# Which DMA ring carries the first weights of a fused layer norm, SSM and SwiGLU kernel, and in which order their first products run

## The chip, the cores and the metric

The kernel runs on one core of a Trainium2 chip. The metric is the device time of one execution in microseconds (us). Times inside an execution come from its profile and are counted from the start of its span; the engines are called as the profile calls them: PE (TensorE, matmuls), DVE (VectorE), ACT (ScalarE), POOL (GpSimd) and SP (SyncE). SPq and ACTq are the instruction streams of SP and ACT in their part as issuers of DMAs; each of the two has a DMA ring of its own.

## The reference

The input `x` has 2048 rows of 512 bf16 values. All matrices are bf16.

```python
xn = _layernorm(x, axis=-1)                       # eps 1e-5, no scale, no shift
# A: a diagonal complex state space layer, 512 states, a scan over the 2048 rows
Bu = einsum("bld,pd->blp", xn, B_bar)
h  = Lam_bar * h + Bu[:, t]                       # for t in 0..2047
yA = 2 * einsum("blp,dp->bld", hseq, Cmat).real + xn * Dskip
# B: SwiGLU, F = 1792
yB = (silu(xn @ w1) * (xn @ w3)) @ w2
return x + yA + yB
```

## The kernel before

The rows are handled in four blocks of 512 (`NBLK`), each of four chunks of 128 rows (c0 to c3 of the first block here). For the products the normalised rows have to stand transposed, 512 features on the partitions in four groups of 128 (`dt` 0 to 3); this is `xnT`. The hidden width 1792 is cut into 14 tiles of 128 (`f`). `glu_up` makes, for each f, a gate product with `w1` (into a PSUM tile `g_ps`) and an up product with `w3` (into `u_ps`); ACT takes both out of PSUM, DVE multiplies. `ssm_in`, the scan tasks and `y_out` do the rest. DVE's tasks of the main part come from a queue with costs in us (`push`, `drain`); nothing of that is touched.

The first block has a head of its own, written out by hand as one program order for each engine (the lines after `stats(0)` at the end of the kernel):

- **Transfers.** SP issues x's chunk c0, then c1 (128 KB each, L77), then four pieces of 256 KB, the first four f tiles of w1 and w3 by halves of the contraction: w1 low (dt 0 and 1), w1 high (dt 2 and 3), w3 low, w3 high (L95); then larger pieces of w1 and w3 (512 and 768 KB), the second block of x, Dskip, and the transposing loads of B. ACT issues four: the first parameter row `Lambda_re` (L109), the chunks c2 and c3 of x in one piece of 256 KB (L77, "the c2/c3 rows" below), and the two other parameter rows. The framework hands eight completion semaphores to the DMAs in turn, so that a ninth DMA is issued when the first has landed, a tenth when the second has, and so on.
- **Dummies.** `keep_warm` (L150) gives PE 8 products of 512 columns and 5 of 128 on constants, while x is on its way, and two of 128 columns later.
- **Normalising.** For each chunk: `stats` and `aggr` on DVE (L164, L167), the reciprocal root on ACT (L171, L172), `normed` on DVE (L192; in two halves for c0 and c1). Then `turn` transposes on PE (L251), two 128-column transposes for a half, and `put` copies the result into `xnT`: on ACT for c0 and c1 (L256, in halves), on DVE for c2 and c3 (L258).
- **First products.** PSUM has eight tiles: three pairs `g_ps`, `u_ps` for f = 0, 1, 2 (`begun`) and two for transposes. The transposes of c1 borrow the pair of f = 2 (`t1`), so the products of f = 2 wait until `put` has read them. `ahead` runs products of the three begun tiles (all L372): w1 low on c0, w1 low on c1, w1 high on c0 and c1 together (256 columns), then w3 low on c0 and c1, the transpose of c2, w3 high, the transposed parameters (L544), and the products on c2 and c3 as those arrive. `glu_up` finishes the three tiles and goes on with f = 3.

PE, like every engine, runs its instructions in this order; one that waits holds up all behind it.

Of the kernel before, what the change touches and what calls it, by code (L numbers as in the profile page):

```python
# [16 lines left out]
P = 128  # L17
# [3 lines left out]
def kernel(  # L21
# [24 lines left out]
    nc = tc.nc  # L46
# [6 lines left out]
    CPB = TBLK // P  # L53
    NSB = TBLK // SB
    NDT = D // P
# [20 lines left out]
    def load_rows(c0, c1, eng):  # L76
        eng.dma_start(out=x_blk[0][:, c0:c1, :], in_=xv[:, 0, c0:c1, :])  # L77
# [4 lines left out]
    w1_sb = const.tile([P, NDT, F], BF16, name="w1_sb")  # L82
    w3_sb = const.tile([P, NDT, F], BF16, name="w3_sb")
    w2_sb = const.tile([P, NFT, D], BF16, name="w2_sb")
    w1v = B_w1.rearrange("(t p) f -> p t f", p=P)
    w3v = B_w3.rearrange("(t p) f -> p t f", p=P)

    H = NDT // 2

    def load_w13(f0, f1, parts=1):  # L90
        fs = slice(f0 * P, f1 * P)
        for w_sb, wv in ((w1_sb, w1v), (w3_sb, w3v)):
            for i in range(parts):
                ds = slice(i * NDT // parts, (i + 1) * NDT // parts)
                nc.sync.dma_start(out=w_sb[:, ds, fs], in_=wv[:, ds, fs])  # L95

    dskip_row = const.tile([P, D], BF16, name="dskip_row")
    bt = [const.tile([P, NDT, PS], BF16, name=f"bt{ri}") for ri in range(2)]
# [5 lines left out]

    prm = const.tile([P, P], BF16, name="prm")
    nc.vector.memset(prm, 0.0)

    def load_prm(i, src, eng):
        eng.dma_start(out=prm[i * NPT:(i + 1) * NPT, :], in_=src.rearrange("(t p) -> t p", p=P))  # L109

    load_prm(0, A_Lambda_re, nc.scalar)
    load_rows(2, CPB, nc.scalar)
    load_prm(1, A_Lambda_im, nc.scalar)
    load_prm(2, A_log_dt, nc.scalar)
    load_w13(0, 4, 2)
    load_w13(4, 8)
    nc.sync.dma_start(out=x_blk[1], in_=xv[:, 1, :, :])
    load_w13(8, NFT)
    nc.sync.dma_start(out=dskip_row, in_=A_Dskip.partition_broadcast(P))
    load_turned(bt[0], A_B_re)  # L120
# [26 lines left out]
    def keep_warm(n, width=512):  # L147
        one = nc.const_aps.tensor_like(1.0, like=ident[:, 0:1])
        for _ in range(n):
            nc.tensor.matmul(out=begun[0][0][:, :width], lhsT=one.to_broadcast([P, P]), rhs=one.to_broadcast([P, width]),  # L150
                             start=True, stop=True)

    keep_warm(8)
    keep_warm(5, P)


    mv_all = const.tile([P, NBLK * CPB, 2], FP32, name="mv_all")
# [4 lines left out]
    def stats(c):  # L162
        sums[c] = work.tile([P, 6], FP32, name="stats", bufs=4)
        nc.vector.bn_stats(out=sums[c], in_=x_blk[c // CPB][:, c % CPB, :])  # L164
# [4 lines left out]
    def rstd_act(c0, c1):  # L169
        y = rstd_all[:, c0:c1]  # L170
        nc.scalar.activation(out=y, in_=mv_all[:, c0:c1, 1], func=ACT.Ln, bias=LN_EPS)  # L171
        nc.scalar.activation(out=y, in_=y, func=ACT.Exp, scale=-0.5)  # L172
# [15 lines left out]
    def normed(c, parts=1):  # L188
        xn = work.tile([P, D], BF16, name="xn", bufs=8)
        for i in range(parts):  # L190
            ds = slice(i * D // parts, (i + 1) * D // parts)
            nc.vector.tensor_scalar(out=xn[:, ds], in0=x_blk[c // CPB][:, c % CPB, ds], scalar1=mv_all[:, c, 0:1],  # L192
                                    scalar2=rstd_all[:, c:c + 1], op0=ALU.subtract, op1=ALU.mult)
        return xn
# [54 lines left out]
    def turn(c, pxt, d0=0, d1=NDT):  # L249
        for dt in range(d0, d1):  # L250
            nc.tensor.transpose(out=pxt[:, dt - d0, :], in_=xn0[c][:, dt * P:(dt + 1) * P], identity=ident)  # L251

    def put(c, pxt, eng, d0=0, d1=NDT):
        dst = xnTs[0][:, d0:d1, c * P:(c + 1) * P]
        if eng is nc.scalar:
            nc.scalar.activation(out=dst, in_=pxt, func=ACT.Copy)  # L256
        else:
            nc.vector.tensor_copy(out=dst, in_=pxt)  # L258
# [110 lines left out]
    def glu_mm(b, f, w_sb, ps, ts, dts=range(NDT), joins=False):  # L369

        for dt in dts:
            nc.tensor.matmul(out=ps[:, ts], lhsT=w_sb[:, dt, f * P:(f + 1) * P], rhs=xnTs[b][:, dt, ts],  # L372
                             start=(dt == 0 and not joins), stop=(dt == NDT - 1))
# [128 lines left out]
    def ahead(w_sbs, fs, c, n=1, dts=range(NDT), joins=False):  # L502
        for f in fs:
            for w_sb in w_sbs:
                glu_mm(0, f, w_sb, begun[f][w_sb is w3_sb], slice(c * P, (c + n) * P), dts, joins)
# [13 lines left out]
    xn0[1] = normed(1, 2)  # L519
    turn(0, tb, H, NDT)  # L520
    put(0, tb, nc.scalar, H, NDT)
    keep_warm(2, P)
    turn(1, t1[0], 0, H)
    put(1, t1[0], nc.scalar, 0, H)
    turn(1, t1[1], H, NDT)
    put(1, t1[1], nc.scalar, H, NDT)
    stats(2)
    aggr(2)
    rstd_act(2, 3)
    stats(3)  # L530
    B3 = (0, 1, 2)
    lo, hi = range(H), range(H, NDT)
    ahead((w1_sb,), B3, 0, 1, lo)
    ahead((w1_sb,), B3, 1, 1, lo, True)
    ahead((w1_sb,), B3, 0, 2, hi)
    xn0[2] = normed(2)
    aggr(3)
    rstd_act(3, 4)
    ahead((w3_sb,), B3, 0, 2, lo)
    turn(2, t2)  # L540
    put(2, t2, nc.vector)
    xn0[3] = normed(3)
    ahead((w3_sb,), B3, 0, 2, hi)
    nc.tensor.transpose(out=pprm, in_=prm, identity=ident)  # L544
# [63 lines left out]
```

## Time and profile before

| | |
|---|---|
| median of 3 runs | 211.74 us (211.68 to 211.76) |
| the profiled execution, its own time | 212.11 us |
| span of the profiled execution | 210.3 us |
| PE busy | 206.6 us (98% of the span), 1036 matmuls |
| DVE, ACT, POOL busy | 173.5, 93.4, 6.0 us |
| chain that ended last | PE 96%, DMA 2% |
| PE idle in 0 to 6.5 us / 6.5 to 13 / 13 to 100 | 1.08 / 0 / 0 us |

The table's last line comes from the view of busy time by stretch (5.42 us busy in the first 6.5, 6.50 in the next 6.5, 87.00 in 87). A row of the timeline gives the start, the time until the last of the merged instructions ended, the engine and line, what is written from what, the shape, the count, and in brackets the idle time before and what ended it. A matmul's own duration includes its way through the pipeline; how fast matmuls follow one another is read from their starts. A DMA row gives its size and the time from issue to landing, that is to the completion of its semaphore.

### The profile page before, as it was taken

How to read it: one execution, taken by the hardware profiler on the slowest of the kernel's cores; microseconds unless marked ns; L12 is line 12 of the kernel's file. 1: busy time of each engine (PE TensorE's matmuls, PEld its weight loads, DVE VectorE, ACT ScalarE, POOL GpSimd, SP SyncE). 2: the span in 40 equal slices, each digit the busy share in tenths (PEclk: the TensorE clock that was granted, in tenths of full speed). 3: DMA queues.
4: the chain of work that ended last, by engine and by line, in shares of the span. 5: the costliest groups of instructions: out<-in, count | busy, mean ns of one | idle time of the engine just before them, and what ended most of it. 6: DMA issues, size and time to landing. Idle time of an engine off the chain costs nothing.

```text
span 210.3 us, 2878 instructions
## 1 busy us (share of the span) xinstructions
PE 206.6 (98%) x1036; PEld 97.7 (46%) x1036; DVE 173.5 (82%) x346; ACT 93.4 (44%) x167; POOL 6.0 (3%) x27
## 2 busy tenths in 40 slices
PE   8999999999999999999999999999999999999994
PEld 3864444444444444444444444444444444444453
DVE  4699989989999999999999999999999999121111
ACT  3599967666666200066666600036666620000000
POOL 2010320000000000000000000000000000000000
PEclk9999999999999999999999999999999999999999
DMA  5999599944000000000004200100000000000110
GB/s 165 294 366 219 109 178 325 217 106 100 0 3 0 0 25 25 28 26 0 0 0 77 28 1 24 50 25 5 0 0 0 0 3 25 27 25 25 34 44 25
DMA packets 25014, 13.69 MB, mean 65 GB/s; under 512 B 15912, under 2 KB 25000, under 8 KB 25000
## 3 DMA queue, kind: packets, MB, share of 16 engines
q1 hardware_dynamic: 24704, 13.24, 26.1%
q10 hardware_dynamic: 296, 0.27, 0.4%
q8 instruction: 8, 0.13, 0.3%
q14 instruction: 6, 0.05, 0.1%
HBM read 7.74 MB, written 2.10 MB: 47 GB/s over the span
## 4 chain that ended last, share of the span: by engine, by line
PE 96%; DMA 2%; SPq 0%; DVE 0%; issue 0%
PE g_ps L372 23%; PE u_ps L372 23%; PE y_ps L488 23%; PE y_ps L493 13%; PE bu_ps L411 13%; DMA w_sb<-in_B_w_dram 2%; SPq L77 0%; PE xt_ps L251 0%; DVE o L498 0%; PE xt_ps L544 0%
## 5 line engine op out<-in xcount | busy, mean ns | idle before, releaser
L372 PEld LDWEIGHTS <-w_sb 128*128 128x128 bf16 x502 | 46.4, 98 | 50.6 <-DMA w_sb<-in_B_w_dram 0.6
L372 PE MATMUL g_ps<-xnT,w_sb 128*128 128x512 bf16 (+2 forms) x254 | 58.2, 354 | 0.3 <-DMA w_sb<-in_B_w_dram 0.3
L372 PE MATMUL u_ps<-xnT,w_sb 128*128 128x512 bf16 (+2 forms) x248 | 58.4, 358 | 0.0
L488 PE MATMUL y_ps<-w_sb,hgT 128*128 128x512 bf16 (+2 forms) x238 | 51.2, 366 | 0.0
L390 ACT ACTIVATE up<-u_ps 128x512 bf16<-128x512 f32 x56 | 34.0, 607 | 14.9 <-PE u_ps L372 14.9
L413 ACT ACTIVATE u<-bu_ps 128x512 bf16<-128x512 f32 x32 | 19.1, 597 | 46.3 <-PE bu_ps L411 46.3
L388 ACT ACTIVATE sl<-g_ps 128x512 bf16<-128x512 f32 x56 | 34.0, 608 | 9.9 <-PE g_ps L372 9.2
L445 DVE TENSOR_TENSOR_SCAN ab<-r_col,h,ab 128x256 bf16<-128x256 f32 x56 | 37.7, 733 | 0.2
L488 PEld LDWEIGHTS <-hgT 128*128 128x128 bf16 x238 | 22.8, 98 | 25.9
L498 DVE TENSOR_TENSOR o<-y_ps,x_blk 128x512 bf16<-128x512 f32 (+2 forms) x17 | 11.1, 654 | 24.3 <-PE y_ps L493 24.3
L493 PE MATMUL y_ps<-ct,h 128*128 128x512 bf16 (+2 forms) x136 | 30.4, 366 | 0.0
L411 PE MATMUL bu_ps<-xnT,bt 128*128 128x512 bf16 x128 | 28.1, 379 | 0.0
L397 DVE TENSOR_TENSOR hgT<-sl,up 128x512 bf16<-128x512 bf16 x56 | 22.9, 414 | 2.1 <-ACT up L390 2.1
L493 PEld LDWEIGHTS <-h 128*128 128x128 bf16 x136 | 13.0, 98 | 14.7
L411 PEld LDWEIGHTS <-bt 128*128 128x128 bf16 x128 | 12.5, 98 | 15.1
L164 DVE BATCH_NORM_STATS2 stats<-x_blk 128x6 f32<-128x512 bf16 x16 | 10.6, 675 | 2.5 <-DMA x_blk<-in_A_x_dram 2.5
L454 DVE TENSOR_TENSOR ab<-ab,tab_s 128x2048 bf16<-128x2048 bf16 x8 | 9.8, 1222 | 0.2
L450 DVE TENSOR_TENSOR ab<-ab,tab_c 128x2048 bf16<-128x2048 bf16 x8 | 9.8, 1222 | 0.1
L427 DVE TENSOR_TENSOR ab<-u,tab_x 128x2048 bf16<-128x2048 bf16 x8 | 9.7, 1219 | 0.0
L430 DVE TENSOR_TENSOR ab<-u,tab_y 128x2048 bf16<-128x2048 bf16 x8 | 9.7, 1218 | 0.0
L201 DVE TENSOR_TENSOR x_blk<-xd,x_blk 128x512 bf16<-128x512 bf16 x16 | 6.8, 426 | 0.5
L200 DVE TENSOR_TENSOR xd<-xn,dskip_row 128x512 bf16<-128x512 bf16 x16 | 6.7, 418 | 0.0
(76 smaller groups left out, 81.3 us busy)
## 6 DMA issues: line engine op xcount, KB each, us to landing
out_dram<-o SPq DMA_DIRECT2D x15, 128.0 KB, 1.7
w_sb<-in_B_w_dram SPq DMA_DIRECT2D x1, 1792.0 KB, 9.3
x_blk<-in_A_x_dram SPq DMA_DIRECT2D x3, 512.0 KB, 6.3
w_sb<-in_B_w_dram SPq DMA_DIRECT2D x2, 768.0 KB, 7.8
w_sb<-in_B_w_dram SPq DMA_DIRECT2D x4, 256.0 KB, 5.0
w_sb<-in_B_w_dram SPq DMA_DIRECT2D x2, 512.0 KB, 4.1
x_blk<-in_A_x_dram SPq DMA_DIRECT2D x2, 128.0 KB, 2.2
x_blk<-in_A_x_dram ACTq DMA_DIRECT2D x1, 256.0 KB, 4.7
```

The lines of the kernel that those rows point to most:

```text
L164: nc.vector.bn_stats(out=sums[c], in_=x_blk[c // CPB][:, c % CPB, :])
L372: nc.tensor.matmul(out=ps[:, ts], lhsT=w_sb[:, dt, f * P:(f + 1) * P], rhs=xnTs[b][:, dt, ts], start=(dt == 0 and not joins), stop=(dt == ...
L388: nc.scalar.activation(out=sl16, in_=g_ps, func=ACT.Silu)
L390: nc.scalar.activation(out=up16, in_=u_ps, func=ACT.Copy)
L397: nc.vector.tensor_tensor(out=hg[b][:, f, :], in0=sl16, in1=up16, op=ALU.mult)
L411: nc.tensor.matmul(out=u_ps, lhsT=bt[ri][:, dt, pt * P:(pt + 1) * P], rhs=xnTs[b][:, dt, :], start=(dt == 0), stop=(dt == NDT - 1))
L413: nc.scalar.activation(out=u16[:, :, pt, ri, :], in_=u_ps.rearrange("p (s t) -> p s t", s=NSB), func=ACT.Copy)
L445: nc.vector.tensor_tensor_scan(out=a[:, pt, 2 * ri + 1, :], data0=r_b, data1=a[:, pt, 2 * ri, :], initial=init, op0=ALU.mult, op1=ALU.add)
L450: nc.vector.tensor_tensor(out=a[:, :, 0::2, :], in0=a[:, :, 1::2, :], in1=tab_b("c"), op=ALU.mult)
L488: nc.tensor.matmul(out=y_ps[:, ds], lhsT=hg[b][:, f, cl * P:(cl + 1) * P], rhs=w2_sb[:, f, ds], start=(f == 0), stop=False)
L493: nc.tensor.matmul(out=y_ps[:, ds], lhsT=h_tiles[i][:, pt, ri, h_ts], rhs=ct[ri][:, pt, ds], start=False, stop=(pt == NPT - 1 and ri == 1))
L498: nc.vector.tensor_tensor(out=o16[:, ds], in0=y_ps[:, ds], in1=x_blk[b][:, cl, ds], op=ALU.add)
```

## The change

ACT's ring now carries w1 low and w1 high and nothing else; everything else of the head goes through SP's ring, the c2/c3 rows and the three parameter rows ahead of w3's pieces. The first of ACT's two issues has to wait for a one-column DVE fill of w1's first column, which the transfer then overwrites. The first `keep_warm` has two more 128-column dummies. The first products run in another order and cut: w1 low on c0 for f = 0 and 1 between the two halves of c1's transposes, then for f = 0 and 1 w1 high on c0, w1 low on c1 and w1 high on c1, each of 128 columns, and then all four contraction groups for f = 2 on c0 and c1 together.

```diff
+    def load_w(w_sb, wv, f0, f1, eng, ds=slice(0, NDT)):
         fs = slice(f0 * P, f1 * P)
+        eng.dma_start(out=w_sb[:, ds, fs], in_=wv[:, ds, fs])
...
     nc.vector.memset(prm, 0.0)
+    nc.vector.memset(w1_sb[:, 0, 0:1], 0.0)
...
-    load_prm(0, A_Lambda_re, nc.scalar)
-    load_rows(2, CPB, nc.scalar)
-    load_prm(1, A_Lambda_im, nc.scalar)
-    load_prm(2, A_log_dt, nc.scalar)
-    load_w13(0, 4, 2)
+    low, high = slice(0, H), slice(H, NDT)
+    load_w(w1_sb, w1v, 0, 4, nc.scalar, low)
+    load_w(w1_sb, w1v, 0, 4, nc.scalar, high)
+    load_rows(2, CPB, nc.sync)
+    load_prm(0, A_Lambda_re, nc.sync)
+    load_prm(1, A_Lambda_im, nc.sync)
+    load_prm(2, A_log_dt, nc.sync)
+    load_w(w3_sb, w3v, 0, 4, nc.sync, low)
+    load_w(w3_sb, w3v, 0, 4, nc.sync, high)
     load_w13(4, 8)
...
     keep_warm(8)
-    keep_warm(5, P)
+    keep_warm(7, P)
...
     turn(1, t1[0], 0, H)
     put(1, t1[0], nc.scalar, 0, H)
+    ahead((w1_sb,), (0, 1), 0, 1, lo)
     turn(1, t1[1], H, NDT)
     put(1, t1[1], nc.scalar, H, NDT)
...
-    ahead((w1_sb,), B3, 0, 1, lo)
-    ahead((w1_sb,), B3, 1, 1, lo, True)
-    ahead((w1_sb,), B3, 0, 2, hi)
+    ahead((w1_sb,), (0, 1), 0, 1, hi)
+    ahead((w1_sb,), (0, 1), 1, 1, lo)
+    ahead((w1_sb,), (0, 1), 1, 1, hi)
+    ahead((w1_sb,), (2,), 0, 2)
```

## The prediction

> **What bounds the kernel now.** I read the page's chain first, then the chain in order of time for the head, then PE's and ACT's timelines around 6 us, then the DMAs.
>
> ```profile
> span 210.3 us, 2878 instructions
> PE 96%; DMA 2%; SPq 0%; DVE 0%; issue 0%
> ```
>
> PE is the chain nearly throughout, and the busy time by stretch shows it without a gap from 6.5 to 100 us. So whatever moves the first products moves the end by as much, unless a later wait takes it back. The chain in order of time says what comes ahead of PE:
>
> ```profile
> 1.64 4.80 DMA w_sb<-in_B_w_dram
> 6.43 0.05 issue
> 6.48 1.51 PE g_ps L372 x18
> 7.99 0.67 PE u_ps L372 x6
> ```
>
> The first product waits for w1 low, issued at 1.64 and landed at 6.43. PE's timeline shows what it had been doing (columns: start, length, what):
>
> ```profile
> 4.88 0.65 PE L251 MATMUL xt_ps<-ident,xn 128*128 128x128 bf16 x4
> 5.33 0.42 PE L150 MATMUL g_ps<-const-bfloat16-1.0 128*128 128x128 bf16 x2
> 5.54 0.42 PE L251 MATMUL g_ps<-ident,xn 128*128 128x128 bf16 x2
> 5.76 0.41 PE L251 MATMUL u_ps<-ident,xn 128*128 128x128 bf16 x2
> 6.48 0.29 PE L372 MATMUL g_ps<-xnT,w_sb 128*128 128x128 bf16 x2 [0.31 <-DMA w_sb<-in_B_w_dram]
> ```
>
> The reader is to see the hole: c1's second transposes start at 5.76 and 5.86, the next instruction at 6.48. ACT shows when the transposed rows are there:
>
> ```profile
> 5.32 0.66 ACT L256 ACTIVATE xnT<-xt_ps 128x256 bf16<-128x256 bf16 x2 [0.25 <-PE xt_ps L251]
> 6.00 0.38 ACT L256 ACTIVATE xnT<-g_ps 128x256 bf16<-128x256 bf16 x1
> 6.28 0.38 ACT L256 ACTIVATE xnT<-u_ps 128x256 bf16<-128x256 bf16 x1
> ```
>
> One such copy takes 0.38, starts 0.28 apart at best: c0 low is there at 5.70, c0 high at 5.98, c1 low at 6.38, c1 high at 6.66. So even with all of w1 present the products could begin only 0.76 earlier, and those on c1 high not before 6.66.
>
> **The change, part by part.** I follow one mark: the start of the first w3 product, 7.83 in PE's timeline before. All behind it is the same in both kernels.
>
> *Rates.* Products of 128 columns follow each other by 0.056 (four take 0.22 from 10.10 on, by their starts), those of 256 by 0.11 (six w3 products from 7.83 to 8.49). Before, w1's part is 12 products of 128 and 6 of 256: 12 x 0.056 + 6 x 0.11 = 1.33. After, f = 0 and 1 take 16 of 128 and f = 2 takes 4 of 256, the same 3072 columns: 16 x 0.056 + 4 x 0.11 = 1.34. No work is gained or lost; only its place counts.
>
> *Dummies.* Two more of 128 columns. The last of the five starts at 4.55, one each 0.11, so two more run to about 4.88, when the first transpose starts after waiting for xn. They lie in that gap: 0. If x came early they would cost 0.2 at most.
>
> *The fill.* 0.06 of DVE (row of the fills at L132, L134), at about 0.86, in DVE's idle time of 1.96 before the first `stats`. ACT's first issue stands at 0.94 now behind the fill of prm; I leave it there. ACT's issues (0.55, then 0.44 by its rows) end near 1.95 instead of 3.16, and ACT's next work is at 3.83: 0.
>
> *w1.* w1 low: 0.94 instead of 1.64. Its landing is bounded below by the fastest row of its kind, the 512 KB piece with nothing else queued (4.1: 5.0) and above by its own 4.8 (5.74). It is wanted at 5.72. Not the bound.
> w1 high: issued at 1.49 instead of 2.11; before, 5.0 to landing, so 7.11. Below: both pieces as one of 512 KB from 0.94, 5.0; above: no sooner than now, 7.1, because the rings share the same bytes per us. I take its own 5.0 from the earlier issue, 6.5.
>
> *The c2/c3 rows and prm.* On SP's ring at 1.64 instead of ACT's at 1.53. Before:
>
> ```profile
> x_blk<-in_A_x_dram ACTq DMA_DIRECT2D x1, 256.0 KB, 4.7
> w_sb<-in_B_w_dram SPq DMA_DIRECT2D x1, 256.0 KB, 4.8
> ```
>
> Both rings served these at one pace. The rows landed at 6.27 when `stats(2)` began; by the same 4.7, 6.35 now. xn of c2 ends at 8.09 (0.41 from 7.68), PE wants it at 8.49: 0.4 of slack, 0.2 of it used up if PE comes 0.2 sooner. The three prm issues took 0.55, 0.38 and 0.27; on SP they stand ahead of w3. They are wanted at 9.37: 0 for themselves.
>
> *w3.* w3 low is issued at 2.11 + 1.20 = 3.3 instead of 2.62, w3 high at 3.75 instead of 3.40 (both also behind the landings of c0 and c1, about 2.9 and 3.4, as now). Latest: 3.3 + 5.2 = 8.5. But the same 1.3 MB stands ahead of it in both kernels, and the DMAs run thin in between:
>
> ```profile
> 2.50:3.00 0.50, 0.50 (x3) 0.21 (x2) 0.11 (x1) 0.00 (x0) 0.00 (x0) 1.00 0.82 258
> 3.00:3.50 0.50, 0.50 (x3) 0.15 (x1) 0.50 (x1) 0.00 (x0) 0.00 (x0) 1.00 0.59 84
> 3.50:4.00 0.50, 0.50 (x2) 0.15 (x1) 0.47 (x3) 0.17 (x1) 0.00 (x0) 1.00 0.59 180
> 4.50:5.00 0.50, 0.48 (x6) 0.21 (x3) 0.50 (x3) 0.34 (x2) 0.00 (x0) 1.00 1.07 373
> ```
>
> The last column is GB/s. From 3 to 4 us 132 pass where 375 could: 0.65 us of transfer lost. w1's earlier issue fills some of it. With half of it won w3 low lands at 2.62 + 5.2 - 0.33 = 7.5; with all of it 7.2. I take 7.5. w3 high (before 8.40, wanted 8.72) likewise has 0.3 to spare.
>
> *Order of the products.* The transposes up to 5.86 follow each other by 0.11, double the 0.056 after 6.48: PE ran at half rate until somewhere between. So w1 low on c0 (four products) starts at 5.72, at 0.11 each, until 6.16; c1's second transposes, now behind them, start at 6.16 and 6.27, the last lasts 0.31 (as before): 6.58. `put` of c1 high 6.60 to 6.98 (now 6.66). w1 high on c1 then starts at 7.00, 0.22, f = 2 0.44: w3 starts at 7.66. By the other wait: w1 high at 6.5 + 0.04, then 12 products x 0.056 and 4 x 0.11 = 1.11: 7.65. The two agree, and w3 low's 7.5 lies ahead of both.
>
> The Trainium skill's page TensorE: Matmul & The Clock Gate (Part 1: The HAM clock gate) puts the change to full rate some 4 us into sustained matmul activity, plus or minus 0.5; PE is busy from 0.76, so by that the early products would run at full rate and, with w1 high there in time, w3 would start near 7.34. The trace disagrees: 5.1 us after 0.76 PE still steps by 0.11. I go by the trace.
>
> *Sum.* 7.83 - 7.66 = 0.17 gained. The first copy at 5.70 hangs on x alone, and ACT's ring now carries w1 while x is in flight; I take 0.03 for that, though it can be much more (third case). 0.14: the profiled execution's span would go from 210.3 to 210.16, its own time from 212.11 to 211.97. The runs' median lies 0.37 under the profiled time; the same difference from 211.74 gives **211.6**.
>
> **The rivals.**
> 1. *As summed*, 0.03 to 0.40 faster: chance 0.55, 211.35 to 211.7.
> 2. *w1 high comes no sooner* (slower). The new order asks for it after four products; the old one asked at 7.28, and it landed at 7.11. From a landing at 7.83 - 1.11 - 0.04 = 6.68 on, each us late is a us lost. For it: the two rings above landed equal pieces 0.16 apart, so w1 may just share with the c2/c3 rows. Against: its issue is 0.62 earlier. At 7.1 w3 starts at 8.25: +0.42, 212.15. Chance 0.13.
> 3. *x comes late.* c0 landed at 2.89 and `stats` began at once; c1 (issued 1.17, 2.2 to landing, 3.4) has 0.3 before its `stats` at 3.71. By the GB/s of quarter us (139, 211, 252 from 1.75 on) c0's 131 KB begin 1.03 after their issue and take until 2.45. So w1 low's begin about 2.0, in the middle of c0's. If c0 then gets half the bytes, its last 0.45 doubles: the head comes 0.45 late, `put` of c1 high ends at 7.43, w3 at 8.11: +0.28, 212.0. It decides from 0.17 on. Chance 0.17. The Trainium skill speaks for this one: DMA: Bandwidth & Descriptors (Issuing engines are not separate DMA queues) says DMAs of all issuers run on the same 16 DMA engines and interleave, so that a second issuer saves issue time alone. The equal landings of the two rings agree.
> 4. *w3 low comes late*, behind three small issues on SP: at 8.5 in the worst case, +0.67, 212.4. SP's issues do wait where a semaphore is still out:
>
> ```profile
> SPq L95 <- DMA w_sb<-in_B_w_dram: 2.7, 1, 2.7
> SPq L95 <- DMA x_blk<-in_A_x_dram: 0.3, 1, 0.3
> ```
>
> Against: the thin stretch. Chance 0.08.
> 5. *All in time*: w1 high by 6.2, full rate by 5.7. c1 high is there at 6.66, w3 starts at 6.68 + 0.22 + 0.44 = 7.34: 0.49 faster, 211.25. This is the ceiling of the whole change. Chance 0.07; it wants w3 low by 7.3 too.
>
> **The numbers.** A difference of 0.2% is 0.42 us, about what a measurement of this kernel can tell from no change. Only case 5 goes beyond it on the fast side, with a part of case 1's tail: 0.09. Case 4 and about half of 2 and a part of 3, where the delays add, go beyond it on the slow side: 0.25. Within: 0.66. The range from 211.3 to 212.25 leaves out most of case 5 and the far ends of 3 and 4, together some 0.2; case 1's own range is 211.35 to 211.7.
>
> **What would show it.** Right: w1 low landed before 5.7 and no wait of PE for it; the first L372 at about 5.7 between c1's two transposes; then one short wait, for w1 high or for the copy of c1 high, near 6.5 to 7.0; the first u_ps product of L372 near 7.65; no wait before the transposes of c2; PE unbroken after that. Wrong: the first `stats` later than 2.9 or the second later than 3.7 (case 3), a wait for w_sb of several tenths before the products of dt 2 and 3 (case 2) or before the first u_ps (case 4), or PE waiting for xn of c2 because the c2/c3 rows land after 6.7. If products step by 0.11 beyond 6.5, the full rate came later than I read, and every product until then costs 0.055 more.

## The result and the profile after

The changed kernel takes **212.41 us** in the median of 14 runs (212.18 to 214.06) against 211.75 (211.58 to 212.15) for the kernel before: 0.66 us more by the medians, and a ratio of 1.0044 with a 95% interval of 1.0031 to 1.0057. Slower, then, where 0.07% faster was forecast, and above the range given. Three of the 14 runs (213.68, 213.75, 214.06) lie apart and lift the ratio; without them the loss is that of the medians. Six single executions of 243.87 to 566.21 us, among the runs below, are left out of every median; two of them were the profiled ones (the rings alone, and the kernel before with four dummies), and those two profiles give no mark. The profiled execution of the changed kernel took 212.31, its span 210.5. (The functions stand 6 to 8 lines lower in the new file: products L378, transposes L257, `stats` L170.)

The chain of the changed kernel in order of time (start, length, what):

```profile
1.17 3.17 DMA x_blk<-in_A_x_dram
4.34 0.02 issue
4.37 0.70 DVE stats L170
...
5.56 0.65 PE xt_ps L257 x4
...
6.92 1.29 PE g_ps L378 x16
8.22 0.66 PE u_ps L378 x6
```

The transfer at the head of the chain is no longer w1 low but c1 of x: issued at 1.17 as before, landed at 4.34 where it had been there by 3.4. The head starts its transposes at 5.56 instead of 4.88. PE's timeline then has no wait for weights at all:

```profile
5.56 0.65 PE L257 MATMUL xt_ps<-ident,xn 128*128 128x128 bf16 x4 [0.49 <-DVE xn L198]
...
6.43 0.38 PE L378 MATMUL g_ps<-xnT,w_sb 128*128 128x128 bf16 x4
...
6.76 1.46 PE L378 MATMUL g_ps<-xnT,w_sb 128*128 128x128 bf16 x16
8.05 0.82 PE L378 MATMUL u_ps<-xnT,w_sb 128*128 128x256 bf16 x6
```

The mark of the prediction, the first w3 product, stands at 8.05 (7.83 in the profile before). The weights did come sooner: w1 low 3.0 after its issue at 0.97, w1 high 4.5 after 1.44, w3's first piece 3.5 after 3.19, 6.7 in place of 7.8. The thin stretch is gone:

```profile
2.50:3.00 0.50, 0.50 (x3) 0.21 (x2) 0.09 (x1) 0.00 (x0) 0.00 (x0) 1.00 0.66 141
3.00:3.50 0.50, 0.50 (x3) 0.15 (x1) 0.50 (x1) 0.00 (x0) 0.00 (x0) 1.00 1.04 367
3.50:4.00 0.50, 0.50 (x2) 0.15 (x1) 0.29 (x2) 0.15 (x1) 0.00 (x0) 1.00 1.13 354
```

367 and 354 GB/s where 84 and 180 had passed. But from 2.5 to 3.0, when c1 should have been moving, it is 141 instead of 258. Which ring moved it is in the queues of 2.5 to 3.25 us (q1 is SP's ring, q10 ACT's; packets, MB, share of the 16 engines). The kernel before:

```profile
q1 hardware_dynamic: 130, 0.11, 48.9%
q10 hardware_dynamic: 30, 0.03, 13.6%
```

The changed kernel, the whole answer for the same stretch:

```profile
q10 hardware_dynamic: 155, 0.16, 76.8%
```

SP's ring, with c1 issued and outstanding, moved not one packet for 0.75 us. ACT's ring moved 32 packets from 1.5 to 2.5 and these 155, all of w1, whose low piece has 256 rows: if these pass in order, c1 began when some 70% of w1 low had passed. From 3.25 to 4.0 the two rings then moved 151 (SP) and 147 (ACT) packets, side by side.

**One relation carries all that follows.** Time of a profiled execution less its mark: 212.11 - 7.83 = 204.28 before, 212.31 - 8.05 = 204.26 after, and 204.25 to 204.30 in nine profiles below whose PE neither waits nor runs at half rate behind the mark. So the end does follow the mark one for one, and a median can be turned into a mark: 211.75 is 7.48, 212.41 is 8.14.

### The profile page after: what moved, and what is told of

Read it like the earlier page. It is cut to its first block, busy times and chain, and to the rows that moved or that the text cites. A ratio compares the mean times of both kernels' runs of the same rounds, so it can differ in the third digit from the quotient of the medians.

```text
span 210.5 us, 2887 instructions
## 1 busy us (share of the span) xinstructions
PE 206.6 (98%) x1040; PEld 98.0 (47%) x1040; DVE 173.5 (82%) x347; ACT 93.4 (44%) x167; POOL 6.0 (3%) x27
## 3 DMA queue, kind: packets, MB, share of 16 engines
HBM read 7.74 MB, written 2.10 MB: 47 GB/s over the span
## 4 chain that ended last, share of the span: by engine, by line
PE 96%; DMA 2%; DVE 1%; SPq 0%; issue 0%
PE g_ps L378 23%; PE u_ps L378 23%; PE y_ps L494 23%; PE y_ps L499 13%; PE bu_ps L417 13%; DMA x_blk<-in_A_x_dram 2%; PE xt_ps L257 1%; DVE stats L170 0%; SPq L77 0%; DVE o L504 0%; DVE xn L198 0%; PE g_ps L156 0%; DVE mv_all L173 0%; PE g_ps L257 0%; PE u_ps L257 0%
## 5 line engine op out<-in xcount | busy, mean ns | idle before, releaser
L378 PEld LDWEIGHTS <-w_sb 128*128 128x128 bf16 x504 | 46.7, 98 | 50.1
L378 PE MATMUL g_ps<-xnT,w_sb 128*128 128x512 bf16 (+1 forms) x256 | 58.6, 353 | 0.0
L378 PE MATMUL u_ps<-xnT,w_sb 128*128 128x512 bf16 (+2 forms) x248 | 58.4, 359 | 0.0
L170 DVE BATCH_NORM_STATS2 stats<-x_blk 128x6 f32<-128x512 bf16 x16 | 10.7, 679 | 2.5 <-DMA x_blk<-in_A_x_dram 2.5
```

## The experiments

Times are medians beside the kernel before in the same job; "+" is their difference, the ratio has its 95% interval.

**The kernel before, once more.**

> The kernel before once more, for a second profile. Its runs lie at 211.58 to 211.83 in 11 of 14, while the profiled execution took 212.11. Theory A (that execution was untypical: a late w1 low): the mark, the first w3 product, stands near 7.45 to 7.5 here, w1 low lands by about 6.1 and PE waits for it by less than 0.1 us. Theory B (it was typical, and the 0.36 us lie elsewhere): w1 low lands at 6.4 again, PE waits 0.3 us, mark at 7.83.

211.88, mark 7.63; w1 low's products start 0.2 earlier than in the first profile:

```profile
6.29 1.50 PE L372 MATMUL g_ps<-xnT,w_sb 128*128 128x128 bf16 x18 [0.29 <-DMA w_sb<-in_B_w_dram]
7.63 0.82 PE L372 MATMUL u_ps<-xnT,w_sb 128*128 128x256 bf16 x6
```

Between the two theories: the mark of this kernel scatters, 7.83 was a late one, the wait for w1 low is real but varies. An estimate for the median: its mark of 7.48 less the 1.35 from first product to mark in the first profile (6.48 to 7.83) puts the first product at 6.13; PE is done with the transposes at 6.00 here and 6.17 there, so the wait is then no more than some 0.1.

**The rings alone** (the new loads, fill and dummies, the old products).

```diff
-    ahead((w1_sb,), (0, 1), 0, 1, lo)
...
-    ahead((w1_sb,), (0, 1), 0, 1, hi)
-    ahead((w1_sb,), (0, 1), 1, 1, lo)
-    ahead((w1_sb,), (0, 1), 1, 1, hi)
-    ahead((w1_sb,), (2,), 0, 2)
+    ahead((w1_sb,), B3, 0, 1, lo)
+    ahead((w1_sb,), B3, 1, 1, lo, True)
+    ahead((w1_sb,), B3, 0, 2, hi)
```

> The new rings, fill and dummies with the old order of the first products. Theory 1 (c1 of x is queued behind w1 low, and all of the loss is there): c1's stats starts near 4.35 as in the changed kernel, the last copy of c1 ends at 6.66 + 0.66 = 7.3, w1 high's 256-column products follow it, mark at 7.3 + 6 x 0.11 = 8.0, time 212.2 to 212.5. Theory 2 (the new cut of the products costs, the rings don't): time as before, 211.7.

212.43, +0.73, ratio 1.0045 (1.0028 to 1.0063): theory 1. The rings do it without the new order. c1's `stats` starts at 4.46 in the profile. One of its six runs took 213.78.

**The order alone** (the reverse of that diff, on the kernel before).

> The new order of the first products with the old rings, no fill, five dummies. Theory 1: c1's stats starts at 3.7; the products of w1 high wait for its landing or for the copy of c1 high behind the slow products, mark at 7.5 to 7.7, time 211.7 to 211.95. Theory 2 (the new cut costs the 0.66): 212.3 to 212.5. Runs more than 1 us over the median: none, if they come from PE's idle 0.49 us in the changed kernel.

211.92, +0.22, ratio 1.0012 (1.0003 to 1.0021):

```profile
5.82 0.40 PE L372 MATMUL g_ps<-xnT,w_sb 128*128 128x128 bf16 x4
6.06 0.27 PE L251 MATMUL u_ps<-ident,xn 128*128 128x128 bf16 x2
6.49 1.28 PE L372 MATMUL g_ps<-xnT,w_sb 128*128 128x128 bf16 x16 [0.16 <-DMA w_sb<-in_B_w_dram]
7.61 0.82 PE L372 MATMUL u_ps<-xnT,w_sb 128*128 128x256 bf16 x6
```

The four early products run, at full rate (starts from 5.82 to 6.00, 0.06 apart), and PE then waits for w1 high, which the new order wants sooner. A small loss of its own.

**c1 ahead of w1 in ACT's ring.**

```diff
-    load_rows(1, 2, nc.sync)
+    load_rows(1, 2, nc.scalar)
```

> The changed kernel with c1 of x issued by ACT ahead of w1 low, in the same ring. Theory 1: c1 no longer queues behind w1, its stats starts at 3.7 right behind c0's, w1 low lands near 4.3, PE does not wait for w_sb, mark near 7.4 to 7.65, time 211.6 to 211.9, no runs more than 1 us over the median. Theory 2 (the cut): still 212.3. Rival 3 of the prediction as it was put (the two rings share the bytes evenly): c0 now lands late as well, its stats at 3.1 to 3.3, and the time is 211.9 to 212.2.

212.14, +0.44, ratio 1.0020 (1.0011 to 1.0029). c1's `stats` is back right behind c0's, at 3.98, PE waits for no weights; but c0's begins at 3.15. Both chunks, issued at once on two rings, land 2.4 and 2.6 after issue instead of 2.2. Theory 1 missed the time; two transfers issued together do delay each other, as rival 3 had it. The profiled execution (211.90, mark 7.63) is 0.24 faster than the median, and what the other runs lost beyond it no profile here shows.

**w1 issued behind c1** (a longer fill first).

```diff
+    pause = const.tile([P, 512], FP32, name="pause")
+    nc.vector.memset(pause, 0.0)
     nc.vector.memset(w1_sb[:, 0, 0:1], 0.0)
```

> The changed kernel with DVE's one-column fill behind a longer fill of a scratch tile (128x512 f32, near 0.5 us), so that ACT issues w1 low near 1.5, behind SP's issue of c1 at 1.17. Theory 1 (what is issued first is served first, and c1's rows wait for all of w1 low): c1's stats starts at 3.7 again, PE does not wait 0.5 for xn, mark (first w3 product) 7.4 to 7.7, time 211.7 to 211.95. Rival (the two rings share evenly whenever both have work): c1 lands about half as late as in the changed kernel, its stats at 4.0, time 212.0 to 212.2.

ACT issues at 1.50. DVE's `stats`:

```profile
2.98 0.69 DVE L172 BATCH_NORM_STATS2 stats<-x_blk 128x6 f32<-128x512 bf16 x1 [1.50 <-DMA x_blk<-in_A_x_dram]
3.81 0.66 DVE L172 BATCH_NORM_STATS2 stats<-x_blk 128x6 f32<-128x512 bf16 x1
```

c1 lands 2.2 after its issue, as in the kernel before, with the same two rings and with the c2/c3 and parameter rows on SP's ring as in the changed kernel: half a microsecond in ACT's issue takes the whole delay away. The time is 212.10, +0.36, ratio 1.0020, over what I expected, because w1 high is now late for the new order (PE waits 0.30 at 6.4, mark 7.80).

**No fill** (its line taken out).

> The changed kernel without the one-column fill, so that ACT issues w1 low near 0.72, together with SP's issue of c0. Theory 1 (order of issue): c0 too is now held back or shares with w1 low, c0's stats later than 3.1, c1's no earlier than 4.3, time 212.4 to 213.2. If the fill is of no use: as the changed kernel, 212.4, c0's stats at 2.9.

212.33, +0.59, ratio 1.0033 (1.0018 to 1.0048). c0's `stats` at 3.37, c1's at 4.46. c0 is late now too, but c1 sets the pace, so the time is no worse than with the fill, and just under the range of theory 1. One of the ten runs took 213.90.

**Half of w1 low ahead of c1**, cut by dt and cut by f.

```diff
-    load_w(w1_sb, w1v, 0, 4, nc.scalar, low)
+    load_w(w1_sb, w1v, 0, 4, nc.scalar, slice(0, 1))
+    load_w(w1_sb, w1v, 0, 4, nc.scalar, slice(1, H))
```

```diff
-    load_w(w1_sb, w1v, 0, 4, nc.scalar, low)
+    load_w(w1_sb, w1v, 0, 2, nc.scalar, low)
+    load_w(w1_sb, w1v, 2, 4, nc.scalar, low)
```

> The changed kernel with w1 low as two transfers of 128 KB, one for each dt, so that half of w1 low (128 rows of 1 KB) stands ahead of c1 instead of 256 rows. Second half issued near 1.45, behind c1. Theory 1: c1 lands about half as late, stats at 3.8 to 4.0 instead of 4.35, time 211.9 to 212.2. If c1's delay is a fixed cost of the second ring: stats at 4.35, 212.4.

> The changed kernel with w1 low as two transfers of 128 KB by f tiles, 256 rows of 512 bytes each. If what holds c1 back is the bytes ahead of it: as with the cut by dt, c1's stats at 3.8 to 4.0. If it is the number of rows (descriptors) ahead of it: c1's stats at 4.3 as in the changed kernel, time 212.4.

Issue to landing of c1, always issued at 1.17, from one profile a row. Other profiles of this document gave 2.0 to 2.1 for the case of the first row and 3.1 to 3.3 for that of the fourth. (`stats` of c1 also has to wait for that of c0, until about 3.7, and so hides up to 0.3 of a delay.)

| ahead of c1 in the other ring | us | `stats` of c1 |
|---|---|---|
| nothing but one parameter row (before) | 2.2 | 3.71 |
| 128 rows of 1 KB | 2.5 | 3.68 |
| 256 rows of 512 bytes | 2.7 | 3.94 |
| 256 rows of 1 KB (the changed kernel) | 3.2 | 4.37 |
| 256 rows of 1 KB, issued 0.33 behind c1 | 2.2 | 3.81 |

c1 waits the longer, the more bytes stand ahead; half of w1 low costs it 0.3 to 0.5 of the 1.0 us. That at equal bytes the rows count too rests on 2.5 against 2.7, no more than the scatter between profiles, and is not shown. The times, 212.85 and 212.42 (ratios 1.0048 and 1.0028), are no measure of that: nine transfers now precede w3's pieces, whose issue moves from 3.19 to 3.67 and 3.94 behind a semaphore, just after c1's landings at 3.67 and 3.87, and PE waits 0.4 and 0.5 for them behind the mark; with the cut by dt it also waits 0.67 for w1 high.

**Two tries at a better kernel.** In the kernel before, ACT's second parameter row ahead of the c2/c3 rows:

```diff
-    load_rows(2, CPB, nc.scalar)
     load_prm(1, A_Lambda_im, nc.scalar)
+    load_rows(2, CPB, nc.scalar)
```

> The kernel before with one swap on ACT's ring: the second parameter row ahead of the c2/c3 rows, whose issue moves from 1.53 to about 1.93, behind SP's issue of w1 low (1.64) and ahead of that of w1 high (2.11). Theory 1 (transfers are served whole, in the order of their issue across both rings): w1 low is no longer behind the c2/c3 rows and lands 0.4 to 0.7 sooner (5.6 to 5.9 against 6.25 to 6.43 in the two profiles of before), the rows land near 6.0, w1 high unchanged; mark (the first w3 product) near 7.3, time 211.5 to 211.7. Rival (the rings share evenly): w1 low lands within 0.2 of before, time 211.7 within 0.1.

211.89, -0.02, ratio 1.0002 (0.9992 to 1.0012). w1 low lands 4.4 after its issue at 1.64, 0.2 to 0.4 sooner than before and so between the two theories, and the first products start at 6.11. But w1 high, issued at 2.10, lands only at 6.96; its products start at 7.01, and the mark stands at 7.74. The rows come later too (`stats` of c2 at 6.32 instead of 5.85 to 6.27) without holding PE up. No gain: the next wait, for w1 high, which theory 1 left out, takes back what w1 low wins.

The later fill with the old order of the products (the two diffs above together):

> The rings of the changed kernel with the later fill (w1 issued by ACT at 1.50, behind c1), and the old order of the first products. Theory 1: w1 low lands near 5.8, w1 high near 6.65 as with the later fill alone; the old order asks for w1 high only after 12 products, so PE waits 0.1 instead of 0.3 for it; mark 7.35 to 7.5, time 211.6 to 211.8, at most 0.1 under the kernel before. If the later fill alone was slow for another reason than the wait for w1 high: 212.1 as there.

```profile
5.97 1.82 PE L380 MATMUL g_ps<-xnT,w_sb 128*128 128x128 bf16 x18
7.63 0.82 PE L380 MATMUL u_ps<-xnT,w_sb 128*128 128x256 bf16 x6
```

211.78, -0.13, ratio 0.9996 (0.9987 to 1.0004). No wait is left in front of the products, x is in time, and it is still not told apart from the kernel before. In this profile PE itself is the limit: it steps by 0.11 until 6.29, the 12 products of w1 low take 1.11 (5.97 to 7.08) where they took 0.79 in the second profile of the kernel before (6.29 to 7.08), and both reach the mark at 7.63. No version here beats it clear of noise.

**The runs near 213.8.** They came in 3 of 14 runs of the changed kernel, and in none of the kernels whose c1 lands in time or nearly so (the kernel before, the order alone, c1 on ACT, both later fills, the later rows, w1 low in halves); the rings alone and the kernel without the fill, whose c1 is late as well, had one each. 14 dummies of 128 columns, none, and at last four of 512 alone, in both kernels:

```diff
-    keep_warm(8)
-    keep_warm(7, P)
+    keep_warm(4)
```

> The changed kernel with 14 dummies of 128 columns instead of 7, so that PE has no idle time of 0.5 us ahead of the first transpose. Theory C (the runs near 213.8, 3 of 14 in the changed kernel, have a clock that goes to full rate one period later because PE idled): median 212.4 as the changed kernel, no run above 213.2. Rival (these runs come from late transfers): some runs near 213.8 again.

> The changed kernel without the 7 dummies of 128 columns: PE idles from about 4.3 to 5.55. Theory C: runs near 213.8 become frequent, a third or more, perhaps all; where the profile is of such a run, the products step by 0.11 instead of 0.056 beyond 7 us. Rival (late transfers): as often as in the changed kernel, some 1 in 5.

> The changed kernel with four dummies of 512 columns and none of 128, so that PE is busy from 0.76 to 2.5 only and idles until the first transpose near 5.55. Theory C (a pause of PE delays the change to full rate): all or most runs near 213.7 to 214.2, and the profile shows products in steps of 0.11 instead of 0.056 until about 9 to 10 us. Rival (the runs near 213.8 come from late transfers): median near 212.3 with some runs above, steps of 0.056 by 6.5 as in the changed kernel.

> The same cut of the dummies in the kernel before, whose c1 is not late. Theory C: here too most runs 1.3 to 2 us over the kernel before, at 213.0 to 213.7, with slow steps beyond 7 us, although no transfer is later than in the kernel before. Rival (late transfers): 211.7 to 211.9, no such runs.

14 dummies: 212.30, +0.39, 0 of 11 such runs, too few to tell from 3 of 14. None of 128: 212.28, +0.37, 3 of 11 (213.43 to 213.96), about as often as in the changed kernel although PE idles 1.22 and not 0.49, which is what the rival had. Four of 512, with 2.95 of idle time: 213.97, +2.22, all four runs there (213.76 to 214.37). In the kernel before: 212.70, +0.95, up to 213.88, less than expected, but with c1 in time (`stats` at 3.61 in the profile). The profile of the changed kernel with four dummies:

```profile
6.43 0.63 PE L377 MATMUL g_ps<-xnT,w_sb 128*128 128x128 bf16 x4
6.86 0.42 PE L256 MATMUL u_ps<-ident,xn 128*128 128x128 bf16 x2
7.07 2.34 PE L377 MATMUL g_ps<-xnT,w_sb 128*128 128x128 bf16 x16
9.21 1.34 PE L377 MATMUL u_ps<-xnT,w_sb 128*128 128x256 bf16 x6
```

The 16 products take 2.34 instead of 1.46; x and the weights land as in the changed kernel (c1's `stats` at 4.37). So a long pause of PE delays the change to full rate, and that alone gives the time of the outlying runs, with no transfer later than in the changed kernel. That the three runs are such cases is possible, not shown: none of them was caught in a profile, and the longer pause of 1.22 did not make them clearly more frequent.

## Why the prediction was wrong, step by step

- *PE is the bound and the mark moves the end*: right, to 0.03 us in eleven profiles.
- *Rates, dummies, the fill*: as put. The issue behind the fill came at 0.97 (0.94 assumed); the dummies cost nothing.
- *w1, the rows, w3*: all sooner than taken: w1 low 4.0 (my range ended at 5.0), w1 high 5.9 (6.5), rows 6.1 (6.35), w3 low 6.7 (7.5). I had sized how long the thin stretch lasts, and it vanished. None of this paid, as PE waited for x.
- *Order of the products*: right in its form, and in its size partly by luck. Worked out for a head in time it gave a mark of 7.66; the order alone stands at 7.61 in its profile and 7.65 by its median (211.92 - 204.27). But there the early products ran at full rate, not at half (the half rate had been read from one execution; in the second profile of the kernel before, the full rate is there from 4.11), so that the copy of c1 high ended at 6.75 and not 6.98; what set the mark was w1 high, there near 6.4 on the old ring, 4.3 after its issue at 2.11, where the prediction had 6.5 from the new ring's earlier issue. In the changed kernel the copy of c1 high, ended at 7.34, sets it: with the 0.02, 0.22 and 0.44 of the prediction 8.02, against 8.05.
- *The base*: failed. I took 7.83 and carried the 0.37 between the profiled time and the median along as a constant. It was no constant: in the second profile w1 low, the very wait that the change aims at, lands 0.18 sooner and the mark stands 0.20 earlier; the rest, from 7.63 to the median's 7.48, no profile shows. Against the median's 7.48 the same 7.66 is 0.18 slower, not 0.17 faster, and the order alone measures +0.22.
- *"I take 0.03 for that"*, for w1 in flight beside x: this is the step that failed most. The third case had the mechanism and a wrong picture of it: even shares from 2.0 on, c0 late by 0.45 and c1 covered by its 0.3. In fact c0 was in time (2.91) and c1, issued 0.2 behind w1 low, stood still until most of that had passed: its `stats` began at 4.37 instead of 3.71, 0.66 late where the term had 0.03. On top of the 7.66 this gave 8.05 in the profile and 8.14 by the median and not 8.32, since the early products and c1's second transposes, now from 6.43 on, no longer ran at half rate. Undoing this delay alone (the later fill) takes back 0.3 of the 0.66; undoing the order as well brings the time back to that of the kernel before.

The Trainium skill's page DMA: Bandwidth & Descriptors (Queues, rings and completion order) has every DMA engine take turns packet by packet between the rings that have work. The 0.75 us without a packet of SP's ring do not look like turns; the 151 and 147 packets of the next 0.75 us do. Whether c1 stood ready in its ring before 3.25 no run here shows, so what held c1 stays open. What is shown is that it depends on the order of issue and on the size of what is ahead.

## What to carry to other kernels

A second DMA ring is no private road: a long transfer issued on it a fifth of a microsecond ahead of a short urgent one can hold the urgent one up until most of it has passed (here 1.0 us for 256 KB ahead of 128 KB), so order the issues of all rings together by need, most urgent first. When a change aims at a wait, look at the wait in more than one execution: the difference between the profiled time and the median may be that wait itself. And give idle PE time at the start its own price, since it can move the change to full rate by microseconds (from about 6.4 to about 10.2 here, with 2.95 us of it).

## What the runs showed of the hardware that was not expected

The change of PE to full rate does not come at one time, though the first dummy starts at 0.76 in every profile. In the first profile of the kernel before, dummies and transposes still step by 0.11 at 5.86; in its second profile the dummies of 128 columns step by 0.06 from 4.11 on, with the later fill (new order) from 3.95 on; with four dummies the change comes between 10.06 and 10.27. The Trainium skill's page TensorE: Matmul & The Clock Gate (Part 1: The HAM clock gate) says that the window in which the activity is counted runs free of the kernel's start, and that the change therefore varies by 0.5 us either way about 4 us. A scatter is there, but a wider one: from at most 3.2 us after the first dummy (later fill) to 5.1 or more (first profile of the kernel before).

The DMAs have thin stretches although transfers are outstanding: in the kernel before 84 GB/s from 3.0 to 3.5 and 98 to 113 from 7.5 to 8.5, against 373 to 386 from 4.5 to 6.0. The 141 GB/s of the changed kernel from 2.5 to 3.0 are such a stretch, and c1 waited through it. What makes them no run here isolates.
